# A decode step with attention and a gated MLP on one core: the MLP as one chain, w_out on 128 and 32 lanes, and output halves as alternate rows of one sum

## The chip, the cores and the metric

The kernel runs on one core of a Trainium2 chip. The metric is the device time of one execution in microseconds (us). Three runs of the kernel before gave 662.22, 662.27 and 662.43 us; the median is 662.27 us. About 0.2% of that, 1.3 us, is what a measurement of this kernel can tell from no change.

## What is computed

Four sequences (B = 4) decode one token each. The input `x` (4 x 640) is normalised; the result goes into an attention over a cache and, beside it, into a gated MLP; both are added to `x`:

```python
xn = layernorm(x)
q  = (xn @ wq) as 4 x 32 heads x 128
p  = softmax(q . k_cache / sqrt(128))        # k_cache, v_cache: 4 x 32 x 4096 x 128, bf16
A  = (p @ v_cache) as 4 x 4096 @ wo          # wo: 4096 x 640
z  = gelu(xn @ w_in)                         # w_in: 640 x 1728, so z is 4 x 2 x 864
B  = (z1 * (w_sp * layernorm(z2) + b_sp)) @ w_out   # w_out: 864 x 640
out = x + A + B                              # 4 x 640
```

The two caches (134 MB each) are nearly all of the bytes that have to be read.

## The kernel before, in words

**Work units.** The attention is cut into 16 units (`NU`): one sequence times eight heads (`hg` is the group of heads, `b` the sequence). The keys of a unit (8192 KB) and its values (8192 KB) are loaded so that each of the 128 partitions holds 64 KB in one run. A unit's keys come in four pieces (`NK`); a step `n` of the main loop handles one piece: VectorE multiplies it by the query in place (`product`, L514) and adds the upper half of the head dimension to the lower (`fold_half`, L520); TensorE adds the rest up with the identity as weights (`sums`, L529, eight matmuls); VectorE finishes the row sums (`row_sums`, L542). After four pieces come the maximum (`head_max`), the exponentials on ScalarE (`exps`, L564), and their spreading by head (`by_head`, L575). The weighted sum of the values is 64 matmuls a unit (`weighted`, L599).

**Places.** The keys live in a ring of seven slots of 2048 KB (`k_ring`), the values in one buffer of 8192 KB (`v_all`). Before the first values come, `v_all` holds the weights `wq`, `w_in` and the first five rows per lane of `w_out`; the other rows of `w_out` stand in `p_m`, which later holds the spread exponentials. `wo` goes into ring slot 4, a quarter of it per group of heads.

**Order.** PE, DVE, Activation and SP run in the written order (`manual_schedule`). All large loads are issued on SP from the list `loads`; `pump()` after each step issues the next ones whose places are free, and SP then waits at each for the readers of that place and for a free completion counter (there are eight, given out in turn). At the start ScalarE issues the load of `x` and five small loads with the last 96 rows of `w_out` (`w_end_sb`, 24 lanes, L115).

**The MLP.** `gmlp()` is a generator that the main loop advances with `next(mlp)`. The 864 features stand as six terms on 128 lanes and four on 24. Its 100 matmuls (L380) run in step 0; its VectorE and ScalarE pieces are dealt out over steps 1 and 2; its last part multiplies with `w_out` (L480: ten terms times two output halves, 20 matmuls).

**The output sum.** The 640 output columns are two halves of 320. Both are summed in one PSUM bank, `out_ps`: half 0 on partitions 0 to 3, half 1 on partitions 32 to 35 (`OG = 32`). Into it go `x` (L355), the MLP (L480), and four times a group of heads (`group_proj`, L668, 8 heads times 2 halves = 16 matmuls):

```python
def out_sum(half):
    return out_ps[OG * half : OG * half + Bsz, :]
...
nc.tensor.matmul(out=out_sum(half), lhsT=o, rhs=wo_sb[:, n, half * NOH : (half + 1) * NOH], ...)
```

**The end.** The last group's `wo` is loaded in six pieces (heads 0-1, 2-3, 4-5, 6, and head 7 in two halves), behind the last values, which come in five (the last four, L167, in falling sizes). After the last value piece: 16 matmuls into `o_last` (L778), their division on VectorE (L786), the 16 matmuls of `group_proj`, one copy of 36 partitions to SBUF on ScalarE (L792), and two stores of 4 x 320, one issued on ScalarE (L793) and one on SP (L794).

Of the kernel before, what the change touches and what calls it, by code (L numbers as in the profile page):

```python
# [9 lines left out]
FP32 = mybir.dt.float32  # L10
BF16 = mybir.dt.bfloat16
# [6 lines left out]
def kernel(  # L18
# [62 lines left out]
    once = ctx.enter_context(tc.tile_pool(name="once", bufs=1))  # L81
# [6 lines left out]

    pad.tile([P, 96], FP32, name="pad")

    p_m = const.tile([P, 2, NG, CB, HT], BF16, name="p_m")
    x_bf = const.tile([Bsz, D], BF16)
    nc.scalar.dma_start(out=x_bf[:], in_=A_x.flatten_outer_dims())

# [6 lines left out]
    w_in_sb = v_all[:, DC * HD : DC * (HD + F)].rearrange("p (c n) -> p c n", c=DC)  # L101


    NV = NFF - 1
    at_v = -(-DC * (HD + F) // 256) * 256
    w_out_sb = v_all[:, at_v : at_v + NV * D].rearrange("p (k n) -> p k n", k=NV)
    p_w = p_m[:].rearrange("p n g c h -> p (n g c h)")
    at_p = -(-D // 256) * 256
    w_row_sb = p_w[:, 0:D]
    w_end_sb = p_w[:, at_p : at_p + FR * D].rearrange("p (r n) -> p r n", r=FR)  # L110
    nc.sync.dma_start(out=wq_sb, in_=A_wq.rearrange("(p c) n -> p c n", c=DC))

    w_end_rows = B_w_out[NFF * P : Fh].rearrange("(p r) n -> p r n", r=FR)
    for l in range(LS):
        nc.scalar.dma_start(out=w_end_sb[l:FT:LS], in_=w_end_rows[l:FT:LS])  # L115

    def load_w():
        nc.sync.dma_start(out=w_in_sb, in_=B_w_in.rearrange("(p c) n -> p c n", c=DC))
        w_rows = B_w_out[0 : NFF * P].rearrange("(p k) n -> p k n", k=NFF)
# [54 lines left out]
    def wo_load(hg):  # L174
        return (lambda: load_wo(hg)), [WO_AT]

    loads = [k_load(0, 0, 2), (load_w, []), k_load(0, 2, 4), k_load(1)]
    for u in range(NU - 4):
        loads += [v_load(u), k_load(u + 2)]
        if u % Bsz == Bsz - 1:  # L180
# [164 lines left out]
        op1=ALU.add,  # L345
    )

    out_ps = ps_out.tile([P, NOH], FP32)
    OG = 32

    def out_sum(half):
        return out_ps[OG * half : OG * half + Bsz, :]

    for half in range(2):
        nc.tensor.matmul(  # L355
            out=out_ps[OG * half : OG * half + OG, :],
            lhsT=ident[:Bsz, :OG],
            rhs=x_bf[:, half * NOH : (half + 1) * NOH],
            start=True,
            stop=False,  # L360
        )

# [7 lines left out]
    gm["yT"] = work.tile([P, NFC, Bsz], BF16, name="yT")  # L370

    def gmlp():
        zz, gw, gt, gz = (gm[n] for n in ("zz", "gw", "gt", "gz"))
        zT = ps_pv.tile([P, 2, NFC, Bsz], FP32, tag="pv", name="zT")
        for t in range(2):
            f1 = t * Fh + NFF * P
            w_t = w_in_sb[:, :, t * Fh : f1].rearrange("p c (f k) -> p c k f", k=NFF)
            for k in range(NFC):
                for c in range(DC):
                    nc.tensor.matmul(  # L380
                        out=zT[: P if k < NFF else FT, t, k, :],
                        lhsT=w_t[:, c, k, :]
                        if k < NFF
                        else w_in_sb[:, c, f1 + k - NFF : f1 + FT * FR : FR],
                        rhs=xnT[:, c, 0:Bsz],
                        start=(c == 0),
                        stop=(c == DC - 1),
                    )
        yield
        nc.vector.tensor_copy(out=zz[:, :, 0:NFF, :], in_=zT[:, :, 0:NFF, :])  # L390
        nc.vector.tensor_copy(out=zz[:FT, :, NFF:], in_=zT[:FT, :, NFF:])
        nc.vector.tensor_tensor(out=gw[:], in0=zz[:], in1=zz[:], op=ALU.mult)
        nc.vector.tensor_scalar(
            out=gw[:], in0=gw[:], scalar1=0.044715, scalar2=1.0, op0=ALU.mult, op1=ALU.add
# [76 lines left out]
            in1=ac_sb[:, None, Bsz : 2 * Bsz].to_broadcast([P, NFC, Bsz]),  # L471
            op=ALU.add,
        )
        nc.vector.tensor_tensor(out=gm["yT"][:], in0=gz[:, 0, :, :], in1=sq, op=ALU.mult)
        w_terms = [w_out_sb[:, k] for k in range(NV)] + [w_row_sb]
        w_terms += [w_end_sb[:FT, r] for r in range(FR)]
        for k in range(NFC):
            w = P if k < NFF else FT
            for half in range(2):
                nc.tensor.matmul(  # L480
                    out=out_sum(half),
                    lhsT=gm["yT"][:w, k, :],
                    rhs=w_terms[k][:, half * NOH : (half + 1) * NOH],
                    start=False,
                    stop=False,
                )
# [151 lines left out]
    def group_turn(hg):  # L638
        rden = small.tile([P, 1], FP32, name="rden")
        nc.vector.reciprocal(out=rden[:], in_=rdens.pop(hg)[:])  # L640


        o_q = gr.pop(hg)[:].rearrange("p (q j) -> p q j", j=JR)
        o_n = once.tile([P, JR, PAR, QH], BF16, name="o_n")
# [9 lines left out]
        o_t = once.tile([P, JR, QD], BF16, name="o_t")  # L654
        nc.vector.transpose(
            out=o_t[:].rearrange("p j q -> p (j q)"),
            in_=o_n[:].rearrange("p j e q -> p (j e q)"),
        )
        o_s = once.tile([P, JR, Bsz], BF16, name="o_s")
        nc.vector.tensor_tensor(  # L660
            out=o_s[:], in0=o_t[:, :, 0:Bsz], in1=o_t[:, :, Bsz : 2 * Bsz], op=ALU.add
        )
        gr[hg] = [o_s[:, j, :] for j in range(JR)]

    def group_proj(hg):
        for n, o in enumerate(gr.pop(hg)):
            for half in range(2):
                nc.tensor.matmul(  # L668
                    out=out_sum(half),
                    lhsT=o,  # L670
                    rhs=wo_sb[:, n, half * NOH : (half + 1) * NOH],
                    start=False,
                    stop=(hg == HG - 1 and n == HT - 1),
                )
        busy.remove(WO_AT)

# [25 lines left out]
    with tc.manual_schedule(engines={E.PE, E.DVE, E.Activation, E.SP}):  # L702
# [74 lines left out]
        for c in range(NC):  # L777
# [4 lines left out]
                start=False,  # L782
                stop=(c == NC - 1),
            )
        o_n = small.tile([P, NQ, PAR, Bsz], BF16, name="o_n_last")
        nc.vector.tensor_tensor(out=o_n[:], in0=o_last[0][:], in1=rden[:], op=ALU.mult)  # L786
        gr[HG - 1] = [o_n[:, h // PAR, h % PAR, :] for h in range(HT)]
        group_proj(HG - 1)

        res = work.tile([P, NOH], BF16, name="res")  # L790
        out_v = out.flatten_outer_dims()
        nc.scalar.copy(out=res[0 : OG + Bsz], in_=out_ps[0 : OG + Bsz])  # L792
# [32 lines left out]
```

## Time and profile before

| what | value |
|---|---|
| device time, median of three runs | 662.27 us |
| span of the profiled execution | 660.5 us |
| median less span | 1.8 us |
| bytes read from HBM | 282.24 MB |
| DVE busy | 524.9 us (79%) |
| PE busy | 310.9 us (47%) |
| ACT busy | 29.8 us (5%) |
| chain that ended last | DMA 60%, DVE 30%, PE 9% |
| the last 16 matmuls of L668 | from 654.73 to 657.64 us |
| copy L792, then stores issued | 657.67 us, 658.12 us |

The page gives no time of its own for the profiled execution beside its span; the three timed runs are about 1.8 us longer than that span, which begins with the first instruction and ends with the last. "Busy" counts an engine's own work, not its waiting. The chain of waits goes back from the last instruction to whatever released each step. The granted clock is the share of full speed that TensorE got: 0.50 is half speed. The view by stretches of time prints, for each stretch, every engine's busy time, the granted clock, the mean busy share of the 16 DMA engines (a packet is booked where it starts, so short stretches can exceed 1.00) and the rate.

### The profile page before, as it was taken

The page shows a single profiled execution, that of the slowest core. Times are in us where ns is not written, and L with a number is a line of the kernel's source. Part 1 is how long each engine was busy: PE and PEld are TensorE (multiplying, and loading weights), DVE is VectorE, ACT ScalarE, POOL GpSimd, SP SyncE. Part 2 cuts the span into 40 slices and gives each one's busy share as a digit, 9 for nine tenths or more (in the row PEclk, how much of TensorE's full clock was granted, in tenths as well). Part 3 has the DMA queues.
Part 4 walks back from the last instruction along what each step waited for, and adds up shares of the span by engine and source line. Part 5 has one row for each costly group of instructions (what it writes and reads, how often), then busy time and mean ns, then how long its engine had stood idle before and what let it go on. Part 6 is the DMA issues. An engine that isn't in the chain of part 4 may idle for free.

```text
span 660.5 us, 4704 instructions
## 1 busy us (share of the span) xinstructions
PE 310.9 (47%) x2035; PEld 135.7 (21%) x2035; DVE 524.9 (79%) x332; ACT 29.8 (5%) x73; POOL 2.7 (0%) x12
## 2 busy tenths in 40 slices
PE   0274363526527362472536336362462633736366
PEld 0131122212203121130212112121130221212124
DVE  2578988959598795969959598695969969999950
ACT  0020000000000000000000000000000000000000
POOL 1000000000000000000000000000000000000000
PEclk9756686766768677576767768677576767678765
DMA  9999999999999999999999999999999999999997
GB/s 372 435 448 429 430 441 437 438 425 437 430 433 438 433 433 438 433 434 425 437 437 438 421 433 438 441 438 433 429 426 441 430 433 445 411 428 437 457 400 281
DMA packets 8113, 282.56 MB, mean 428 GB/s; under 512 B 888, under 2 KB 2180, under 8 KB 2588
## 3 DMA queue, kind: packets, MB, share of 16 engines
q1 hardware_dynamic: 8024, 282.12, 99.0%
q8 instruction: 16, 0.26, 0.1%
q10 hardware_dynamic: 68, 0.13, 0.1%
q14 instruction: 5, 0.04, 0.0%
HBM read 282.24 MB, written 0.01 MB: 427 GB/s over the span
## 4 chain that ended last, share of the span: by engine, by line
DMA 60%; DVE 30%; PE 9%; issue 1%; ACT 0%; DVEq 0%; SPq 0%
DMA k_ring<-in_A_k_cache_dram 52%; DVE k_ring L514 15%; DVE k_ring L520 8%; PE s_ps L529 7%; DMA v_all<-in_A_v_cache_dram 4%; DMA k_ring<-in_A_wo_dram 3%; DVE s_sb L542 2%; DVE p_m L575 1%; DVE m L551 1%; PE out_ps L668 1%; DVE o_n L646 1%; PE zT L380 1%; PE pv L599 1%; DVE mt L553 0%; PE out_ps L480 0%
## 5 line engine op out<-in xcount | busy, mean ns | idle before, releaser
L514 DVE TENSOR_TENSOR k_ring<-k_ring,qbc 128x8192 bf16<-128x8192 bf16 x64 | 282.7, 4418 | 86.3 <-DMA k_ring<-in_A_k_cache_dram 86.3
L529 PE MATMUL s_ps<-k_ring,ident 128*128 128x512 bf16 x512 | 201.1, 564 | 313.7 <-DVE k_ring L520 313.5
L529 PEld LDWEIGHTS <-ident 128*128 128x128 bf16 x512 | 65.4, 129 | 427.7 <-issue 383.7
L520 DVE TENSOR_TENSOR k_ring<-k_ring 128x4096 bf16<-128x4096 bf16 x64 | 145.9, 2279 | 0.0
L599 PE MATMUL pv<-v_all,p_m 128*32 128x512 bf16 x960 | 60.2, 407 | 0.0
L542 DVE TENSOR_REDUCE s_sb<-s_ps 128x64 f32<-128x512 f32 x64 | 43.6, 682 | 5.7 <-PE s_ps L529 5.7
L575 DVE TENSOR_TENSOR p_m<-p_c,own 128x2048 bf16<-128x2048 bf16 x16 | 36.5, 2284 | 0.7 <-ACT p_c L564 0.7
L599 PEld LDWEIGHTS <-p_m 128*32 128x32 bf16 x992 | 25.8, 103 | 39.4 <-issue 17.1
L564 ACT ACTIVATE p_c<-s_sb,nm 128x256 bf16<-128x256 f32 x16 | 8.1, 508 | 331.2 <-DVE nm L558 331.2
L630 PEld LDWEIGHTS o_ps<-o_rows,pick 128*128 128x128 f32 x96 | 19.5, 280 | 4.1 <-issue 3.0
L630 PE MATMUL o_ps<-o_rows,pick 128*128 128x128 f32 x96 | 18.6, 357 | 0.0
L611 ACT COPY o_rows<-pv 128x512 f32<-128x512 f32 x16 | 9.4, 586 | 167.4 <-PE pv L599 167.4
L293 DVE TENSOR_SCALAR q_rows<-q_ps 128x512 bf16<-128x512 f32 x2 | 1.4, 692 | 12.3 <-PE q_ps L285 12.3
L786 DVE TENSOR_TENSOR o_n_last<-o_last,rden_all 128x32 bf16<-128x32 f32 x1 | 0.2, 192 | 12.3 <-PE o_last L778 12.3
L504 ACT CAST qbc<-qbc_ps 128x128 bf16<-128x128 f32 x16 | 4.3, 266 | 101.7 <-PE qbc_ps L496 101.7
L285 PE MATMUL q_ps<-v_all,xnT 128*32 128x512 bf16 x40 | 4.3, 618 | 8.9 <-DMA v_all<-in_A_wq_dram 8.9
L551 DVE TENSOR_REDUCE m<-s_sb 128x1 f32<-128x256 f32 x16 | 6.7, 420 | 0.6
L496 PE MATMUL qbc_ps<-q_rows,of_row 128*128 128x128 bf16 x32 | 6.0, 277 | 0.6 <-DVE q_rows L293 0.6
L496 PEld LDWEIGHTS <-of_row 128*128 128x128 bf16 x32 | 4.2, 134 | 8.3 <-issue 7.8
L668 PE MATMUL out_ps<-k_ring,o_s 128*4 128x320 bf16 x48 | 4.4, 331 | 2.2 <-DVE o_s L660 2.2
L685 PE MATMUL o_last<-hot,o_rows 128*128 128x8 f32 x32 | 4.9, 280 | 0.7 <-ACT o_rows L611 0.7
L685 PEld LDWEIGHTS o_last<-hot,o_rows 128*128 128x128 f32 x32 | 4.8, 225 | 1.8 <-ACT o_rows L611 1.6
(89 smaller groups left out, 74.6 us busy)
## 6 DMA issues: line engine op xcount, KB each, us to landing
k_ring<-in_A_k_cache_dram SPq DMA_DIRECT2D x6, 4096.0 KB, 24.8
v_all<-in_A_v_cache_dram SPq DMA_DIRECT2D x2, 4096.0 KB, 28.8
v_all<-in_A_wq_dram SPq DMA_DIRECT2D x1, 5120.0 KB
k_ring<-in_A_v_cache_dram SPq DMA_DIRECT2D x1, 4096.0 KB
k_ring<-in_A_wo_dram SPq DMA_DIRECT2D x3, 1280.0 KB, 20.1
v_all<-in_B_w_in_dram SPq DMA_DIRECT2D x1, 2160.0 KB
k_ring<-in_A_v_cache_dram SPq DMA_DIRECT2D x1, 2048.0 KB
k_ring<-in_A_v_cache_dram SPq DMA_DIRECT2D x1, 1024.0 KB
```

The lines of the kernel that those rows point to most:

```text
L496: nc.tensor.matmul(out=qb_ps[:], lhsT=of_row[:, e, b].rearrange("p k f l -> p (k f l)"), rhs=q_rows[e][:, hg, :], start=(e == 0), stop=(e ...
L514: nc.vector.tensor_tensor(out=t, in0=t, in1=qbcs[u][:, None, :].to_broadcast([P, HC, Dh]), op=ALU.mult)
L520: nc.vector.tensor_tensor(out=t[:, :, 0:HD2], in0=t[:, :, 0:HD2], in1=t[:, :, HD2:Dh], op=ALU.add)
L529: nc.tensor.matmul(out=s[:], lhsT=ident[:], rhs=t[:, :, g * RW : (g + 1) * RW], start=(g == 0), stop=(g == m - 1),)
L542: nc.vector.tensor_reduce(out=scores[u][:, r * HC : (r + 1) * HC], in_=sums_ps.pop(n)[:], axis=AX.X, op=ALU.add,)
L551: nc.vector.tensor_reduce(out=m1[:], in_=scores[u][:], axis=AX.X, op=ALU.max)
L575: nc.vector.tensor_tensor(out=p_m[:, u % 2], in0=p_c.pop(u)[:].rearrange("p (g c) -> p g c", c=CB)[:, :, :, None].to_broadcast([P, NG, CB, HT]
L599: nc.tensor.matmul(out=pvs[u][cg * QD : (cg + 1) * QD, :], lhsT=p_m[:, u % 2, g0 + n].rearrange("p c h -> p (c h)"), rhs=v_at[:, n * CB : ...
L611: nc.scalar.copy(out=o[:].rearrange("p c d -> p (c d)"), in_=pvs.pop(u)[:])
L630: nc.tensor.matmul(out=gr[hg][:], lhsT=pick[:, c, Bsz - 1 - b : P + Bsz - 1 - b], rhs=o[:, c, :], start=(b == 0 and c == 0), stop=(b == Bs ...
L668: nc.tensor.matmul(out=out_sum(half), lhsT=o, rhs=wo_sb[:, n, half * NOH : (half + 1) * NOH], start=False, stop=(hg == HG - 1 and n == HT ...
L685: nc.tensor.matmul(out=o_last[0][:, :, :, u % Bsz], lhsT=o[:, c, :], rhs=hot[:, c, :].rearrange("p (k e) -> p k e", e=PAR), start=(c == 0) ...
```

## The change

Four things change together.

1. **Terms of the MLP.** The 864 features are now five terms on 128 lanes (`FA`) and seven on 32 (`FB`, `FL`): 12 terms in place of 10, so 120 matmuls with `w_in` and 24 with `w_out`. The 640 first rows of `w_out` are one load into `v_all`; the 224 others are four loads of 8 rows into `p_m` (`load_w_b`, on SP), behind the second half of the first keys. ScalarE's five small loads and SP's load of one row per lane are gone.
2. **First keys.** The first load of keys (two pieces, 4096 KB) is split in two of 2048 KB.
3. **One chain.** All of the MLP behind its first matmuls is done in step 1, after the second fold; `row_sums` of steps 0 and 1 stand between its parts. `v_all` is free for the first values after step 1 in place of step 2.
4. **Output sum.** `out_ps` has eight rows, row 2b + half. Each matmul has eight weight columns: a sequence's column stands at every second place of a tile with zeros between (`x_at`, `yT`, `o_s`, cleared by GpSimd at the start), and the two halves use the same tile shifted by one. All matmuls write partitions 0 to 7. One copy of eight partitions and one store of 8 x 320, issued on ScalarE, end the kernel.

Two small tiles of `group_turn` move into the end of `p_m`'s buffer. The diff, cut to what matters (`...` marks what is left out):

```diff
-    NFF = Fh // P
-    FR = 4
-    FT = (Fh - NFF * P) // FR
-    NFC = NFF + FR
-    LS = 5
+    FA, FL, LS = 5, 32, 4
+    FB = (Fh - FA * P) // FL
+    NFC = FA + FB
...
-    for l in range(LS):
-        nc.scalar.dma_start(out=w_end_sb[l:FT:LS], in_=w_end_rows[l:FT:LS])
+    def load_w_b():
+        for l in range(LS):
+            nc.sync.dma_start(out=w_b_sb[l:FL:LS], in_=w_b_rows[l:FL:LS])
...
-        nc.sync.dma_start(out=w_out_sb, in_=w_rows[:, 0:NV])
-        nc.sync.dma_start(out=w_row_sb, in_=w_rows[:, NV])
+        nc.sync.dma_start(
+            out=w_a_sb, in_=B_w_out[0 : FA * P].rearrange("(p k) n -> p k n", k=FA)
+        )
...
-    loads = [k_load(0, 0, 2), (load_w, []), k_load(0, 2, 4), k_load(1)]
+    loads = [k_load(0, 0, 1), k_load(0, 1, 2), (load_w, []), k_load(0, 2, 4), (load_w_b, []), k_load(1)]
...
-    out_ps = ps_out.tile([P, NOH], FP32)
-    OG = 32
-    def out_sum(half):
-        return out_ps[OG * half : OG * half + Bsz, :]
+    OR = 2 * Bsz
+    out_ps = ps_out.tile([OR, NOH], FP32)
+    def at_half(w, half):
+        return w[:, 1 - half : 1 - half + OR]
...
-                    out=out_sum(half),
-                    lhsT=o,
+                    out=out_ps[:],
+                    lhsT=at_half(o, half),
                     rhs=wo_sb[:, n, half * NOH : (half + 1) * NOH],
                     start=False,
-                    stop=(hg == HG - 1 and n == HT - 1),
+                    stop=(hg == HG - 1 and n == HT - 1 and half == 1),
...
-            if n in (1, 2):
-                next(mlp)
-            if n:
+            if n > 2:
                 row_sums(n - 1)
...
             if n == 1:
                 next(mlp)
-            if n in (1, 2):
+                row_sums(0)
                 next(mlp)
...
-            if n == 2:
+            if n == 1:
+                next(mlp)
+                row_sums(1)
+                next(mlp)
+                next(mlp)
                 busy.remove(V)
...
-        nc.scalar.copy(out=res[0 : OG + Bsz], in_=out_ps[0 : OG + Bsz])
-        nc.scalar.dma_start(out=out_v[:, 0:NOH], in_=res[0:Bsz])
-        nc.sync.dma_start(out=out_v[:, NOH:D], in_=res[OG : OG + Bsz])
+        nc.scalar.copy(out=res[:], in_=out_ps[:])
+        nc.scalar.dma_start(
+            out=out.flatten_outer_dims().rearrange("b (h n) -> (b h) n", h=2), in_=res[:]
+        )
```

More of the change, by code (lines that the diff above doesn't have):

```diff
@@ L346 @@
     )
-    out_ps = ps_out.tile([P, NOH], FP32)
-    OG = 32
-    def out_sum(half):
-        return out_ps[OG * half : OG * half + Bsz, :]
+    OR = 2 * Bsz
+    out_ps = ps_out.tile([OR, NOH], FP32)
+    def at_half(w, half):
+        return w[:, 1 - half : 1 - half + OR]
+    x_at = const.tile([Bsz, OR + 1], BF16, name="x_at")
+    nc.gpsimd.memset(x_at[:], 0.0)
+    nc.gpsimd.tensor_copy(out=x_at[:, 1::2], in_=ident[:Bsz, :Bsz])
+    yT = const.tile([P, NFC, OR + 1], BF16, name="yT")
+    nc.gpsimd.memset(yT[:], 0.0)
+    o_s = const.tile([P, JR, OR + 1], BF16, name="o_s")
+    nc.gpsimd.memset(o_s[:], 0.0)
     for half in range(2):
         nc.tensor.matmul(
-            out=out_ps[OG * half : OG * half + OG, :],
-            lhsT=ident[:Bsz, :OG],
+            out=out_ps[:],
+            lhsT=at_half(x_at, half),
             rhs=x_bf[:, half * NOH : (half + 1) * NOH],
-            start=True,
+            start=(half == 0),
             stop=False,
@@ L369, with lanes @@
     gm["ac"] = work.tile([1, 2 * Bsz], FP32, name="ac")
-    gm["yT"] = work.tile([P, NFC, Bsz], BF16, name="yT")
+    def lanes(k):
+        return P if k < FA else FL
     def gmlp():
@@ L375, in gmlp @@
         for t in range(2):
[L376 to L377 removed]
+            w_t = w_in_sb[:, :, t * Fh : (t + 1) * Fh]
             for k in range(NFC):
+                w_k = (
+                    w_t[:, :, k : FA * P : FA]
+                    if k < FA
+                    else w_t[:, :, FA * P + k - FA : Fh : FB]
+                )
                 for c in range(DC):
                     nc.tensor.matmul(
[L381 to L384, printed above, removed]
+                        out=zT[0 : lanes(k), t, k, :],
+                        lhsT=w_k[:, c],
                         rhs=xnT[:, c, 0:Bsz],
@@ L389, in gmlp @@
         yield
-        nc.vector.tensor_copy(out=zz[:, :, 0:NFF, :], in_=zT[:, :, 0:NFF, :])
-        nc.vector.tensor_copy(out=zz[:FT, :, NFF:], in_=zT[:FT, :, NFF:])
+        nc.vector.tensor_copy(out=zz[:, :, 0:FA, :], in_=zT[:, :, 0:FA, :])
+        nc.vector.tensor_copy(out=zz[:FL, :, FA:], in_=zT[:FL, :, FA:])
         nc.vector.tensor_tensor(out=gw[:], in0=zz[:], in1=zz[:], op=ALU.mult)
@@ L473, in gmlp @@
         )
-        nc.vector.tensor_tensor(out=gm["yT"][:], in0=gz[:, 0, :, :], in1=sq, op=ALU.mult)
-        w_terms = [w_out_sb[:, k] for k in range(NV)] + [w_row_sb]
-        w_terms += [w_end_sb[:FT, r] for r in range(FR)]
+        nc.vector.tensor_tensor(out=yT[:, :, 1::2], in0=gz[:, 0, :, :], in1=sq, op=ALU.mult)
+        w_terms = [w_a_sb[:, k] for k in range(FA)] + [w_b_sb[:, r] for r in range(FB)]
         for k in range(NFC):
-            w = P if k < NFF else FT
             for half in range(2):
                 nc.tensor.matmul(
-                    out=out_sum(half),
-                    lhsT=gm["yT"][:w, k, :],
+                    out=out_ps[:],
+                    lhsT=at_half(yT[0 : lanes(k), k], half),
                     rhs=w_terms[k][:, half * NOH : (half + 1) * NOH],
@@ L653, in group_turn @@
             )
-        o_t = once.tile([P, JR, QD], BF16, name="o_t")
+        o_t = p_end[:, JR * QD : 2 * JR * QD].rearrange("p (j q) -> p j q", j=JR)
         nc.vector.transpose(
-            out=o_t[:].rearrange("p j q -> p (j q)"),
-            in_=o_n[:].rearrange("p j e q -> p (j e q)"),
+            out=p_end[:, JR * QD : 2 * JR * QD], in_=p_end[:, 0 : JR * QD]
         )
-        o_s = once.tile([P, JR, Bsz], BF16, name="o_s")
         nc.vector.tensor_tensor(
-            out=o_s[:], in0=o_t[:, :, 0:Bsz], in1=o_t[:, :, Bsz : 2 * Bsz], op=ALU.add
+            out=o_s[:, :, 1::2], in0=o_t[:, :, 0:Bsz], in1=o_t[:, :, Bsz : 2 * Bsz], op=ALU.add
         )
-        gr[hg] = [o_s[:, j, :] for j in range(JR)]
+        gr[hg] = [o_s[:, j] for j in range(JR)]
     def group_proj(hg):
@@ L668, in group_proj @@
                 nc.tensor.matmul(
-                    out=out_sum(half),
-                    lhsT=o,
+                    out=out_ps[:],
+                    lhsT=at_half(o, half),
                     rhs=wo_sb[:, n, half * NOH : (half + 1) * NOH],
                     start=False,
-                    stop=(hg == HG - 1 and n == HT - 1),
+                    stop=(hg == HG - 1 and n == HT - 1 and half == 1),
                 )
@@ L784 @@
             )
-        o_n = small.tile([P, NQ, PAR, Bsz], BF16, name="o_n_last")
-        nc.vector.tensor_tensor(out=o_n[:], in0=o_last[0][:], in1=rden[:], op=ALU.mult)
-        gr[HG - 1] = [o_n[:, h // PAR, h % PAR, :] for h in range(HT)]
-        group_proj(HG - 1)
-        res = work.tile([P, NOH], BF16, name="res")
-        out_v = out.flatten_outer_dims()
-        nc.scalar.copy(out=res[0 : OG + Bsz], in_=out_ps[0 : OG + Bsz])
-        nc.scalar.dma_start(out=out_v[:, 0:NOH], in_=res[0:Bsz])
-        nc.sync.dma_start(out=out_v[:, NOH:D], in_=res[OG : OG + Bsz])
+        nc.vector.tensor_tensor(
+            out=o_s[:, :, 1::2],
+            in0=o_last[0][:].rearrange("p k e b -> p (k e) b"),
+            in1=rden[:].rearrange("p k e b -> p (k e) b"),
+            op=ALU.mult,
+        )
+        gr[HG - 1] = [o_s[:, h] for h in range(HT)]
+        group_proj(HG - 1)
+        res = work.tile([OR, NOH], BF16, name="res")
+        nc.scalar.copy(out=res[:], in_=out_ps[:])
+        nc.scalar.dma_start(
+            out=out.flatten_outer_dims().rearrange("b (h n) -> (b h) n", h=2), in_=res[:]
+        )
 _INS = ['A_x', 'A_k_cache', 'A_v_cache', 'A_wq', 'A_wo', 'B_x', 'B_w_in', 'B_w_sp', 'B_b_sp', 'B_w_out']
```

20 lines of the change are left out of this document (9 added, 11 removed).

## The prediction, made before the changed kernel ran

> **What bounds the kernel now.** I read the stretches of time first, because the chain of waits gives DMA 60% but DVE 30%, and a chain can run through an engine that holds nothing up.
>
> ```profile
> 1.00:41.00 40.00, 13.30 (x159) 7.81 (x159) 15.87 (x22) 3.39 (x5) 2.20 (x7) 0.79 1.00 419
> 41.00:81.00 40.00, 18.05 (x58) 6.34 (x59) 36.72 (x40) 4.17 (x8) 0.00 (x0) 0.59 1.02 439
> 81.00:121.00 40.00, 19.22 (x110) 8.42 (x110) 34.47 (x19) 1.45 (x4) 0.00 (x0) 0.67 1.00 433
> 121.00:621.00 500.00, 235.50 (x1435) 100.50 (x1434) 421.33 (x240) 18.63 (x51) 0.00 (x0) 0.70 1.00 433
> 621.00:655.00 34.00, 22.39 (x265) 11.79 (x264) 16.32 (x15) 1.77 (x4) 0.00 (x0) 0.65 0.98 413
> ```
>
> The second number from the right is the busy share of the DMA engines: 1.00 from 1 us on, to within a few us of the end. Packet by packet the trace says the same: a 64 KB packet takes 2.418 us on its engine, in any stage, and the next starts at once; I found no pause of 0.2 us on any of the 16 engines between the first packet (1.7 us) and their last loads. So work on DVE and PE costs nothing as long as the queues never run dry. What can move the time is the bytes of the slowest DMA engine, a queue that runs dry, and what follows the last landings. That end I read next, in the chain of waits from 600 us on (start, length, what):
>
> ```profile
> 607.98 26.36 DMA v_all<-in_A_v_cache_dram
> ...
> 634.36 21.95 DMA k_ring<-in_A_wo_dram
> ...
> 656.35 1.30 PE out_ps L668 x8
> ...
> 657.67 0.42 ACT res L792
> ```
>
> Then the last matmuls one by one in the timeline of PE:
>
> ```profile
> 654.73 0.43 PE L668 MATMUL out_ps<-k_ring,o_n_last 128*4 128x320 bf16 x2 [0.28 <-DVE o_n_last L786]
> 656.35 0.43 PE L668 MATMUL out_ps<-k_ring,o_n_last 128*4 128x320 bf16 x2 [0.17 <-DMA k_ring<-in_A_wo_dram]
> 656.57 0.48 PE L668 MATMUL out_ps<-k_ring,o_n_last 128*4 128x320 bf16 x2
> ```
>
> "x2" is the point. The two halves of a head start 3 to 7 ns apart and run side by side; the next pairs start at 656.57, 656.84 and 657.11. A pair costs 0.267 us, not each matmul. PE keeps step with the landings of `wo`: the pairs at 655.49 and 656.35 waited for theirs, and so did the very last half (657.21). The last packet of `wo` lies at 656.8 us.
>
> **The change part by part.**
>
> *Output rows (the part that costs).* Both halves now write partitions 0 to 7, with eight weight columns each. Within one half, before, successive heads write the same partitions and start 0.267 us apart (0.22 only for the first behind a pause; 0.136 in the group at 389.11, at full clock). I take that as the step between any two matmuls to the same rows: 0.267 us at the clock of 0.50 which the end gets. Bounds: the halves still overlap (0.133 each) or not at all (0.267); the row for two matmuls on the same partitions is the nearer one, so 0.267. Their weight loads (80 to 129 ns) lie under the product before, as they do now. The tail then is 16 x 0.267:
> - it starts where it starts now, 654.73, behind the division L786 (0.19 us; its output has a stride now, I add nothing);
> - the last of 16 starts 15 x 0.267 = 4.01 us later, at 658.73. The pieces of `wo` all land before their turn (the last at 657.2), so PE bounds the tail, not the landings;
> - before, the last one started at 657.21. Both ends add the same 0.43 us. Cost: 658.73 - 657.21 = **+1.52 us**.
>
> The other places are covered. `group_proj` of the first three groups grows from 1.25 us (16 at full clock) or 1.85 us (230.87) to 2.2 to 4.3 us. Behind it on SP stands a load of keys that needs slot 4 (issued 232.76 and 390.40), which comes up to 2.4 us later. Those loads land 26.9 and 28.0 us after their issue, and 8192 KB at 433 GB/s take 19.4, so more than 7 us of other bytes are queued ahead: hidden. On PE, the next `sums` wait for a product and a fold anyway (4.42 + 2.28 us).
>
> *One copy, one store.* The copy reads 320 numbers on eight partitions in place of 36: 0.42 us as now, since the free size is the same. Two stores become one of eight rows. ScalarE's store is seen done at 659.43, SP's at 659.61, so at most 0.18 us goes; a store of eight rows may take as much longer as the issue of 5-row loads (0.62 to 0.79 us) does over that of this 4-row store (0.28), but a 128-row issue takes 0.33. Bounds -0.2 and +0.3; I take **-0.1**, nearest to the two stores themselves.
>
> *w_out and first keys on the DMA engines.* By the packet records: before, 24 rows of 5120 B came five at a time, on at most five engines (up to 5 x 0.196 us each), and 128 rows of 1280 B on all (8 x 0.055). That is 1.42 us on the loaded engines and 0.44 on the others. Now 32 rows of 8960 B come eight at a time: four on each of eight engines, each between 0.309 (8192 B) and 0.385 (10240 B), say 0.338, so 1.35 us, and nothing on the other eight. The split keys replace 8 x 1.213 by 16 x 0.611 us, +0.07 everywhere. The loaded engines stay at 1.42. Others gain 0.37 or lose 0.98, and which of them ends last I can't tell. Bounds -0.4 and +1.0; I take **0.0**, the value for the engines loaded in both.
> [...]
>
> *One chain, earlier start.* The first piece of keys now lands about 4.8 us earlier (2048 KB at 433 GB/s), so the first product starts when the query is ready (22.1) in place of 26.11. The fold and `sums` follow (2.28 + 3.57): SP issues the second keys near 32.5, not 36.52. Then 120 matmuls of 0.042 us (L380) to about 38, the MLP's vector pieces, `sums` of step 1 in between, and 24 products of `w_out` at 0.267 (6.4 us, not 2.92), from about 47.5 to 54. The ten that read `v_all` are done near 50.4, where SP may issue the first values: 56.92 before. Step 2 starts near 47.5 in place of 55.25. Every load is issued earlier than now, at queues that didn't run dry before. The four small loads stand ahead of the second keys on SP; each waits for a completion counter of a load that has landed by about 27 us, before 32.5. **0.0**: nothing waits for the gain. Without that cover (queues dry at 56 us) it would be worth up to the 6 us by which the values come earlier.
>
> Sum against the profiled execution: 660.5 + 1.52 - 0.1 + 0.0 = 661.9. Times stand 1.8 us above that span: 662.27 + 1.42 = **663.7 us**, 0.21% slower.
>
> [...]
>
> **Rivals.**
>
> *The clock is released in the tail* (not slower). Rows: in the group at 389.11, 16 matmuls as eight pairs took 1.25 us at full clock. Sixteen single ones at 0.136 would start within 15 x 0.136 = 2.0 us, by 656.8, before the last landing at 657.2; then the landings bound the tail again and only the -0.1 stays: 662.2. For it: after `sums` began at 568.95, 586.57 and 600.84 the granted clock rose to 1.00 within 3.3 to 4.5 us, and the tail is now dense. Against: the products of L778 kept PE 90% busy from 648 to 652 us and the clock stayed at 0.50. It decides by when the release comes: at 658.0, the earliest by those delays, about 0.4 us is saved (663.3); from 0.1 us saved on the result is within 0.2%; for 662.2 it must come by about 656.
> [...]
>
> *A newly loaded DMA engine ends last*: +0.98 before the tail, so 664.7; the opposite, 663.3. Against the extreme: the ends differ by 3 us between engines, so one has to be near the last already.
>
> *A queue that runs dry early*, if the single-file products or small loads hold up the first values beyond 60 us: some us slower. Nothing in the order says so.
>
> *The start matters after all* (a hidden gap): up to 6 us faster. The packet records speak against it.
>
> **How the numbers follow.** Forecast (serial tail at half clock, 663.2 to 664.2): 0.58. Clock released in the tail or halves partly together (662.2 to 663.2): 0.20. DMA engine or small fetches later (664.2 to 664.9): 0.14. Dry queue 0.04, faster start 0.04. The range from 662.4 to 664.8 leaves out the last two and the ends of the others, about 0.15. The bound of 0.2% (1.32 us, about what a measurement can tell from no change) is at 663.6, inside the forecast: about 0.4 of its 0.58 lies above it. Slower 0.40 + 0.14 + 0.04 = 0.58; faster 0.04; within 0.38.
>
> **What would show it.** Right: 16 matmuls of the last `group_proj` start 0.267 us apart and end near 659.2, without waiting for `wo`; the first values are issued about 6 us earlier and the DMA share still reads 1.00 throughout. Wrong: starts in pairs; a clock of 1.00 after 658; a last landing of the values' pieces that differs from 653.8 by more than 0.5 us; a DMA share under 0.95 in the first 80 us.

## The result, and the profile after

The changed kernel takes **664.10 us** (median of nine runs, 663.52 to 664.55); the kernel before took 662.27 us beside it (nine runs, 662.19 to 662.55). The ratio is 1.0024, with an interval of 1.0016 to 1.0033: slower by 1.8 us. The forecast was 663.7 us. The profiled execution has a span of 661.7 us (660.5 before) and a device time of 663.52 us, so it is the shortest of the nine; this matters below.

The stretches of time of the changed kernel, with the columns that the prediction showed (busy time and count of PE, PEld, DVE, ACT and POOL, granted clock, DMA share, GB/s):

```profile
1.00:41.00 40.00, 15.54 (x181) 9.75 (x181) 20.35 (x30) 4.95 (x7) 2.59 (x11) 0.78 0.99 416
41.00:81.00 40.00, 20.12 (x64) 7.54 (x63) 34.88 (x31) 2.62 (x7) 0.00 (x0) 0.71 1.01 438
81.00:121.00 40.00, 18.32 (x109) 7.77 (x108) 32.53 (x18) 1.45 (x4) 0.00 (x0) 0.67 1.02 440
121.00:621.00 500.00, 238.94 (x1433) 103.45 (x1431) 420.77 (x240) 18.63 (x51) 0.00 (x0) 0.70 1.00 433
621.00:655.00 34.00, 22.44 (x262) 11.07 (x260) 16.70 (x15) 1.77 (x4) 0.00 (x0) 0.65 0.98 412
```

The DMA share is what it was, 0.98 to 1.02 in every stretch, although DVE's work has moved forward (20.35 us of it by 41 us, 15.87 before). The queues of large loads were full before the change and they still are. The early start shows in the timeline of SP, which issues the second keys (L146) and the first values (L157). First the changed kernel, then the first values in the kernel before:

```profile
31.98 0.34 SPq L146 DMA_DIRECT2D k_ring<-in_A_k_cache_dram  x1
50.20 0.33 SPq L157 DMA_DIRECT2D v_all<-in_A_v_cache_dram  x1
```

```profile
56.92 0.33 SPq L157 DMA_DIRECT2D v_all<-in_A_v_cache_dram  x1
```

The values are issued 6.7 us earlier, and nothing of it reaches the end. The end itself, in the chain of waits (start, length, what):

```profile
612.48 41.82 DMA k_ring<-in_A_v_cache_dram
...
654.34 0.61 PE o_last L787 x16
...
654.98 0.21 DVE o_s L794
...
655.23 3.77 PE out_ps L675 x16
...
659.02 0.42 ACT res L804
```

Before, the chain ran through `wo` up to 656.31 and then through eight products. Now `wo` is no longer in it: it goes from the last values through the division and then through all 16 products in one unbroken run. The first and the last of these in the timeline of PE:

```profile
655.23 0.69 PE L675 MATMUL out_ps<-k_ring,o_s 128*8 128x320 bf16 x2 [0.29 <-DVE o_s L794]
```

```profile
657.86 1.13 PE L675 MATMUL out_ps<-k_ring,o_s 128*8 128x320 bf16 x6
```

Behind the first step of 0.22 us the starts are 0.267 us apart (one by one in the trace: 655.46, 655.72, 655.99 and so on to 658.12); then come 658.28, 658.41, 658.55 and 658.69, 0.136 apart. Six products begin within 0.83 us in the second fence, which single file at 0.267 would not allow. The stretches of PE alone (PE busy, granted clock, DMA share, GB/s) say why:

```profile
656.00:657.00 1.00, 1.00 (x5) 0.50 0.19 63
657.00:658.00 1.00, 1.00 (x5) 0.50 0.02 7
658.00:659.00 1.00, 0.98 (x7) 0.92 0.00 0
```

The clock came back at 658.16 (0.92 is the mean of 0.16 us at 0.50 and 0.84 us at 1.00). Term by term, in us:

| in the profiled runs | before | changed |
|---|---|---|
| start of the last group of `o_last` | 653.85 | 654.34 |
| first of the 16 products | 654.73 | 655.23 |
| start of the last one | 657.21 | 658.69 |
| its end | 657.64 | 658.99 |
| end of the copy to end of the span | 2.39 | 2.30 |
| span | 660.49 | 661.74 |

From first to last start it is 2.485 us before and 3.455 now: +0.97. In the profile of e6, below, where the clock stayed at 0.50, it is 3.96 us; so the clock saved 0.50 us here. The tail starts 0.50 us later, which the prediction had at zero, so that in this profile the two cancel.

### The profile page after: what moved, and what is told of

It reads as the page before. It is cut to its first block, busy times and chain, and to the rows that moved or that the text cites. A ratio compares the mean times of both kernels' runs of the same rounds, so it can differ in the third digit from the quotient of the medians.

```text
span 661.7 us, 4753 instructions
## 1 busy us (share of the span) xinstructions
PE 319.1 (48%) x2059; PEld 141.3 (21%) x2059; DVE 525.6 (79%) x332; ACT 29.8 (5%) x73; POOL 3.1 (0%) x16
## 4 chain that ended last, share of the span: by engine, by line
DMA 62%; DVE 29%; PE 8%; issue 1%; SPq 0%; ACT 0%; DVEq 0%
DMA k_ring<-in_A_k_cache_dram 53%; DVE k_ring L523 15%; DVE k_ring L529 7%; DMA k_ring<-in_A_v_cache_dram 6%; PE s_ps L538 6%; DMA v_all<-in_A_wq_dram 2%; DVE s_sb L551 2%; DVE p_m L584 1%; PE out_ps L675 1%; DVE m L560 1%; PE q_ps L285 1%; DVE p_m L655 1%; DVE mt L562 1%; DVE mt L565 0%; DVE nm L567 0%
## 5 line engine op out<-in xcount | busy, mean ns | idle before, releaser
L675 PE MATMUL out_ps<-k_ring,o_s 128*8 128x320 bf16 x64 | 11.2, 336 | 2.2 <-DVE o_s L667 1.9
L675 PEld LDWEIGHTS <-o_s 128*8 128x8 bf16 x64 | 5.8, 96 | 7.1 <-DVE o_s L667 2.7
L393 PE MATMUL zT<-xnT,v_all 128*32 128x4 bf16 (+1 forms) x120 | 6.2, 188 | 0.0
L393 PEld LDWEIGHTS <-v_all 128*32 128x32 bf16 (+1 forms) x120 | 6.2, 141 | 0.0
```

What stands on the lines that cost most here:

```text
L393: nc.tensor.matmul(out=zT[0 : lanes(k), t, k, :], lhsT=w_k[:, c], rhs=xnT[:, c, 0:Bsz], start=(c == 0), stop=(c == DC - 1),)
L675: nc.tensor.matmul(out=out_ps[:], lhsT=at_half(o, half), rhs=wo_sb[:, n, half * NOH : (half + 1) * NOH], start=False, stop=(hg == HG - 1 a ...
```

## The experiments

All were run in three groups, each beside the kernel before on the same chip, whose medians were 662.33 (18 runs), 662.31 (22) and 662.27 us (19). Times are medians with their extremes. "Lost DMA time" below is the time that packets of SP's queue took beyond what a packet of that size usually takes, as a mean over the 16 engines. It is added up from the packet records of the traces and stands in no view.

**e1, the changed kernel without the output rows.** Halves on partitions 0 and 32 again, two stores; all else is as changed.

```diff
+    def out_sum(half):
+        return out_ps[OG * half : OG * half + Bsz, :]
+    def cols(w):
+        return w[:, 1:OR:2]
...
-                    out=out_ps[:],
-                    lhsT=at_half(o, half),
+                    out=out_sum(half),
+                    lhsT=cols(o),
```

> The changed kernel with its output halves put back on partitions 0 and 32 (four weight columns each, two copies' rows, two stores); first keys, w_out split and MLP chain stay as changed. Theory (single-file products in the tail cost the time): the last pairs wait for wo again, starts in pairs 0.27 us apart, and the time falls from 664.1 by 1.2 to 1.8 us, to between 662.3 and 662.9; the upper end if the last landings stay about 0.5 us later than before, as in the profile of the changed kernel, the lower end if that was chance. Rival (the MLP chain, the split keys or the new w_out loads cost it): stays near 664.

Measured: 662.70 us (662.46 to 662.91), ratio 1.0003 (0.9994 to 1.0011). The 16 products in the timeline of PE are pairs again (two of them begin 2 to 7 ns apart, all but the last two); first the first pair, then all 16:

```profile
655.08 0.43 PE L679 MATMUL out_ps<-k_ring,o_s 128*4 128x320 bf16 x2 [0.29 <-DVE o_s L798]
```

```profile
655.08 2.92 PE L679 MATMUL out_ps<-k_ring,o_s 128*4 128x320 bf16 x16 [0.29 <-DVE o_s L798]
```

They take 2.92 us in all, first start to last end, with pauses for `wo`; single file they took 3.77 with the clock's help. With the rows away no slowdown above the interval is left: of the 1.83 us between the medians 1.40 went with the rows, and 0.37 that the interval does not tell from nothing stayed.

**e2, the kernel before with the output rows alone** (rows 2b + half, shifted tiles, one copy, one store; loads and MLP as before).

```diff
...
-                    out=out_sum(half),
-                    lhsT=o,
+                    out=out_ps[:],
+                    lhsT=at_half(o, half),
...
```

> The kernel before with only the output rows and the one store of the change (loads, MLP terms and chain as before). Theory: the 16 last products start singly 0.267 us apart from 654.7 on, +1.52 us, less up to 0.55 us where the clock of TensorE is released on the way, less 0.2 us for the store: 663.0 to 663.6. Rival (the loads and the chain cost the time, the rows nothing): 662.0 to 662.3.

Measured: 664.09 us (663.64 to 665.53), ratio 1.0029 (1.0019 to 1.0039). That is 0.5 us above the range that was expected, and as much as the whole change. Its chain of waits ends with

```profile
654.27 0.61 PE o_last L783 x16
...
655.16 4.45 PE out_ps L673 x16
```

Here the clock returned only at 659.85, and the 16 products took 4.45 us, 0.68 more than in the profile of the changed kernel. From first to last start it is 3.96 us, +1.47 over the kernel before. The other 0.4 us is a later tail: its last group of `o_last` starts at 654.27 in place of 653.85. The rows have a second place in this kernel, the products with `w_out` in the old order of the MLP. First the ten that read `v_all` in e2 and the issue of the first values behind them, then the same ten in the kernel before:

```profile
55.24 2.83 PE L486 MATMUL out_ps<-v_all,yT 128*8 128x320 bf16 x10 [2.94 <-DVE yT L480]
...
58.10 0.33 SPq L157 DMA_DIRECT2D v_all<-in_A_v_cache_dram  x1
```

```profile
55.39 1.50 PE L480 MATMUL out_ps<-v_all,yT 128*4 128x320 bf16 x10 [2.72 <-DVE yT L474]
```

In single file they free `v_all` later, and the first values are issued 1.2 us later than before. In the packet records the DMA engines are then idle for 0.13 us on average between 60.5 and 62 us, where the kernel before has no gap, and 17 packets of 64 KB that start between 59.1 and 63.4 take 2.51 to 3.38 us in place of 2.418. Of the lost DMA time of e2 between 50 and 150 us (0.54 us, 0.11 in the kernel before) 0.43 us lies there. Idle and lost time together, 0.56 us, agree with the later tail in size; this is read from one profile and was not tested by a run.

**e6, the changed kernel once more, and e8, the kernel before once more** (no edit; second profiles of both).

> The changed kernel once more, for a second profile of its tail and its time on the chip of these runs. If its spread (663.5 to 664.6) comes from where the clock of TensorE is released among the 16 products: the step between products is 0.267 us up to the release and 0.136 us behind it, and the profiled run's time moves with it, by up to 0.55 us. Rival (the spread comes from the landings): products alike in both profiles and the last landing of values moves.

> The kernel before once more, for a second profile. If the last values land up to 0.5 us apart from run to run by chance: the last group of L778 starts between 653.8 and 654.4. If the later landings of the changed kernel come from its loads: again 653.8 to 653.9.

Measured: e6 664.04 us (663.33 to 664.11), ratio 1.0022 (1.0012 to 1.0032); e8 662.16 us in one run, span 660.37. The last group of `o_last` starts at 654.27 in e6 and at 653.73 in e8, which is what e8 was expected to show if the loads of the change delay the landings. The profiled run of e6 took 664.11 us, and its stretches of PE read

```profile
657.00:658.00 1.00, 1.00 (x5) 0.50 0.01 3
658.00:659.00 1.00, 1.00 (x5) 0.50 0.00 0
659.00:660.00 1.00, 0.59 (x3) 0.50 0.00 0
660.00:661.00 1.00, 0.00 (x0) 0.98 0.02 5
```

```profile
655.16 4.43 PE L675 MATMUL out_ps<-k_ring,o_s 128*8 128x320 bf16 x16 [0.29 <-DVE o_s L794]
```

The clock stayed at 0.50 to 660.03, behind the last product. So the two profiles of one kernel show the two cases that the prediction had set apart. Without the clock's help the serial term can be read whole: first to last start is 3.96 us in e6 and 2.49 in e8, **+1.47** (forecast +1.52). The spans differ by 1.95 us: +0.55 from the later start of the tail (655.16 against 654.61), +1.47, +0.04 in the last product and -0.11 behind the copy.

**e7, two stores of four rows** in place of one of eight, on ScalarE and SP.

```diff
-        nc.scalar.dma_start(
-            out=out.flatten_outer_dims().rearrange("b (h n) -> (b h) n", h=2), in_=res[:]
-        )
+        out_v = out.flatten_outer_dims().rearrange("b (h n) -> (b h) n", h=2)
+        nc.scalar.dma_start(out=out_v[0:Bsz], in_=res[0:Bsz])
+        nc.sync.dma_start(out=out_v[Bsz:OR], in_=res[Bsz:OR])
```

> The changed kernel with two stores of four rows, on ScalarE and SP, in place of one of eight rows; all else as changed. Theory (one store saves the later end of two): 0.1 to 0.25 us slower than the changed kernel, 664.2 to 664.4, seen as the time from the end of the copy to the end of the span. Rival (eight rows take as long as two stores): no difference.

Measured: 664.03 us (663.65 to 664.09), ratio 1.0024 (1.0014 to 1.0034). It was expected to be slower, at 664.2 to 664.4; in the device time the store cannot be told from no change. In the profiles, end of copy to end of span is 2.37 to 2.57 us in the seven runs with two stores (before, e1, e5, e7, e8, e9, e11) and 2.21 to 2.34 in the seven with one (changed, e2, e3, e4, e6, e10, e12). The medians are 0.15 us apart, about as forecast; e7, whose stores alone differ from those of the changed kernel, has 2.37 against 2.30 and 2.29, so 0.07 to 0.08. The profile of e7 is also a third one of the single-file tail: 3.96 us from first to last start, and the clock stays at 0.50 to the end of the span at 662.29.

**e10, twice the products, single file.** In the last group each product has one with zero weights (`o_z`) ahead of it, which adds nothing to the sum.

```diff
...
+            for half in range(2 if hg == HG - 1 else 0):
+                nc.tensor.matmul(
+                    out=out_ps[:],
+                    lhsT=at_half(o_z, half),
+                    rhs=wo_sb[:, n, half * NOH : (half + 1) * NOH],
+                    start=False,
+                    stop=False,
+                )
```

> The changed kernel, and in the last group each of the 16 output products has one more ahead of it with zero weights, which adds nothing to the sum: 32 products in single file. Theory (products to the same eight rows follow each other, 0.267 us apart at the clock of 0.50 and 0.136 at full clock, and PE alone bounds the tail): in the two profiles of the changed kernel the clock came back 2.9 and 4.9 us after the first product of the tail. 4 us at 0.267 are 15 products, the other 17 at 0.136 take 2.3 us, so the last one starts about 6.3 us behind the first in place of 3.0 to 4.0: 2.0 to 2.8 us over the changed kernel, about 666.4; 4.3 us, 668.3, if the clock does not come back. Rival (the tail is bound by the landings of wo or by what each product waits for, not by the products): less than 0.5 us more, 664.1 to 664.6.

**e11, the same in pairs**: e1 with a zero pair ahead of each pair.

> The changed kernel with the halves on partitions 0 and 32 and two stores (as in e1), and in the last group each pair of products has a pair with zero weights ahead of it: again 32 products, but as 16 pairs. Theory (a pair takes the time of one product): 16 pairs are as long as the 16 single products of the changed kernel, so 662.7 + 1.5 = 664.2 us (663.6 if the clock comes back early), and 2 to 2.8 us below the same 32 products in single file. Rival (it is the number of products or the bytes they read that counts, and the pairs of before were only waiting for wo): the time of the 32 in single file, about 666.4.

Measured: e10 665.45 us (665.26 to 666.00), ratio 1.0048 (1.0034 to 1.0062); e11 664.10 us (663.57 to 664.38), ratio 1.0025 (1.0015 to 1.0034). From the timeline of PE, first e10, then e11 (here the zero products are L677 and L681):

```profile
656.49 0.74 PE L685 MATMUL out_ps<-k_ring,o_s 128*8 128x320 bf16 x2
657.03 0.74 PE L677 MATMUL out_ps<-k_ring,o_z 128*8 128x320 bf16 x2
...
660.07 0.43 PE L677 MATMUL out_ps<-k_ring,o_z 128*8 128x320 bf16 x2
660.34 0.43 PE L685 MATMUL out_ps<-k_ring,o_s 128*8 128x320 bf16 x2
```

```profile
656.46 0.48 PE L689 MATMUL out_ps<-k_ring,o_s 128*4 128x320 bf16 x2
656.72 0.48 PE L681 MATMUL out_ps<-k_ring,o_z 128*4 128x320 bf16 x2
...
658.86 0.48 PE L681 MATMUL out_ps<-k_ring,o_z 128*4 128x320 bf16 x2
659.12 0.48 PE L689 MATMUL out_ps<-k_ring,o_s 128*4 128x320 bf16 x2
```

Two products to the same rows take 0.53 to 0.54 us at the clock of 0.50 (656.49 to 657.03) and 0.27 at full clock; two products to rows on partitions 0 and 32 (e11) take 0.26 to 0.27 at 0.50, from end to end of the run. The same number of products, reading the same bytes of `wo`, is 1.35 us shorter in pairs, and 16 pairs (664.10) are as long as the 16 single products of the changed kernel (664.10 and 664.04); from first to last start 16 pairs take 3.96 us in e11 and 16 single products 3.96 in e6. So the cost follows the place of the output, not the count of the products or their reads. The two also differ in weight columns, eight in single file and four in pairs. No run has eight columns with the halves on partitions 0 and 32; but with four columns successive pairs, which go to the same rows again, start 0.267 us apart in e11 (655.390, 655.657, 655.924), the step that eight columns have, so the number of columns does not set it. The size for e10 was missed: +1.4 us over the changed kernel and not 2.0 to 2.8, since the clock came back earlier than in either profile I had reckoned from, at 657.67, 2.7 us behind the first product, and 20 of the 31 steps were at 0.136. For the same reason e11 is 1.35 us below e10 and not 2 to 2.8; its own time, 664.2, was met.

**e5, the loads of the kernel before evened out**: the last 96 rows of `w_out` on 96 lanes as one load, in place of 24 lanes in five loads.

```diff
-    FR = 4
+    FR = 1
...
-    LS = 5
+    LS = 1
```

> The kernel before with the last 96 rows of w_out as one term on 96 lanes in place of four on 24: one load of 96 rows of 1280 B for five loads of 24 rows of 5120 B; 70 and 14 matmuls of the MLP, not 100 and 20. Every DMA engine then moves 6 rows (0.33 us), where up to five engines moved 5 rows of 5120 B (0.98 us) and the others none. If the loaded engines end last in the kernel before: up to 0.65 us faster, 661.7 to 662.1. Rival (others end last, or engines even out): from no change to 0.33 us slower, 662.2 to 662.6.

Measured: 662.36 us (662.11 to 663.59), ratio 1.0004 (0.9995 to 1.0013). The few engines reckoned to carry 1.42 us of small loads (5 x 0.196 + 8 x 0.055) were not the ones that the end waited for, or evening them is worth less than 0.1%.

**e9, e1 with even loads** (six terms on 128 lanes, one on 96; one load of 96 rows).

```diff
-    FA, FL, LS = 5, 32, 4
+    FA, FL, LS = 6, 96, 1
...
-            out=w_a_sb, in_=B_w_out[0 : FA * P].rearrange("(p k) n -> p k n", k=FA)
+        nc.sync.dma_start(out=w_a_sb, in_=w_rows[:, 0 : FA - 1])
+        nc.sync.dma_start(out=w_row_sb, in_=w_rows[:, FA - 1])
```

> As e1 (changed kernel with pairs and two stores), but with w_out on 128 and 96 lanes: six terms and one, one load of 96 rows in place of four of eight, and one row per lane by its own load, as before. Theory A (the 0.4 us that e1 has over the kernel before come from the DMA engines that the small loads load more): 662.3. Theory B (they come from the split of the first keys or from the order of the loads): 662.7. Theory C (they are chance): anything between.

Measured: 662.55 us (662.33 to 662.73), ratio 1.0003 (0.9994 to 1.0012). It falls between theories A and B, as C (chance) allowed, and with this noise it rules none of them out. The last wait for `wo` ends at 656.35 before, 656.18 in e5, 656.69 in e1 and here at

```profile
634.46 21.98 DMA k_ring<-in_A_wo_dram
...
656.48 1.28 PE out_ps L681 x8
```

The last values differ with them, by up to 0.5 us; no experiment ties this to one part of the change.

**e3, the changed kernel with two loads of 16 rows, and e12, with one of 32**, in place of four of eight.

```diff
-    FA, FL, LS = 5, 32, 4
+    FA, FL, LS = 5, 32, 2
```

> The changed kernel with the 32 rows of w_out loaded as two loads of 16 rows in place of four of 8, so that each row goes to another DMA engine: 2 rows on each of 16 engines, 0.68 us, not 4 rows on 8, 1.35 us. If the load of those engines delays the last landings: landings and time earlier by 0.3 to 0.7 us, 663.4 to 663.8. Rival (the 0.5 us in the landings is chance, or the loaded engines don't end last): 664.1, within 0.2.

> The changed kernel with one load of 32 rows of w_out in place of four of eight: 16 engines, two rows each, all at once. Theory A (16 engines that write into the same 32 partitions slow each other, which made e3 with its two loads slower): packets of 8960 bytes of 0.37 us and more, slow packets behind them, 664.7 us or more. Theory B (it was the order of the two loads, one behind the other, or chance): packets of 0.34 us, no lost engine time, 663.6 to 664.2.

Measured: e3 664.91 us (664.17 to 665.04), ratio 1.0035 (1.0022 to 1.0047); e12 664.75 us (663.93 to 665.03), ratio 1.0033 (1.0020 to 1.0046). These loads were meant to lie evenly on sixteen engines, and the time goes up, against both expectations of e3. The stretch around these loads, first in the changed kernel, then in e3, then in e12:

```profile
41.00:46.00 5.00, 3.36 (x11) 1.04 (x9) 2.18 (x11) 0.31 (x2) 0.00 (x0) 0.72 1.21 523
```

```profile
41.00:46.00 5.00, 3.89 (x10) 1.15 (x10) 1.79 (x9) 0.59 (x2) 0.00 (x0) 0.63 1.27 455
```

```profile
41.00:46.00 5.00, 3.49 (x10) 1.04 (x8) 2.18 (x11) 0.40 (x2) 0.00 (x0) 0.70 1.25 452
```

The DMA engines are busier (1.27 and 1.25 against 1.21) and move less (455 and 452 GB/s against 523). The packets of 8960 bytes all take 0.338 us with four loads; with two they have a median of 0.373 and reach 0.644, with one 0.443 and 0.664, and 16 or 17 of the 64 KB packets near them take up to 3.6 and 3.7 us in place of 2.418. The lost DMA time between 30 and 50 us is 1.12 and 1.09 us, against 0.03 in the changed kernel. The last group of `o_last` starts 0.68 us later in e12 (655.02 against 654.34) and 0.26 later in e3. So the loss repeats, and two loads in a row are not its cause, since one load has it too; the medians alone (0.65 and 0.8 us over the changed kernel, with ranges that overlap) would not show it. That the short rows are what slows the 64 KB packets is not shown: most of the loss is in these, and in e4, below, 16 such packets are slowed about as much with no more than four short rows at a time. What slows the short rows themselves, to 0.644 and 0.664 us, no run shows either.

**e4, eight loads of four rows.**

```diff
-    FA, FL, LS = 5, 32, 4
+    FA, FL, LS = 5, 32, 8
```

> The changed kernel with the same rows as eight loads of 4 rows: 8 rows on each of four engines, 2.7 us in place of 1.35. If the load of an engine goes straight into the end of the stream: up to 1.35 us later, 664.8 to 665.5. Rival (engines even out, or other engines end last): 664.1 to 664.4.

Measured: 667.12 us (666.27 to 667.28), ratio 1.0067 (1.0053 to 1.0081). It lies far above both expectations: it was meant as a dose of loaded engines and became something else. SP's timeline and the stretch behind it:

```profile
25.73 17.94 SPq L115 DMA_DIRECT2D p_m<-in_B_w_out_dram  x6
43.80 0.35 SPq L146 DMA_DIRECT2D k_ring<-in_A_k_cache_dram  x1
```

```profile
41.00:46.00 5.00, 3.67 (x10) 1.15 (x10) 1.96 (x10) 0.58 (x2) 0.00 (x0) 0.67 0.78 270
```

The last of the small loads is not issued before 43.09; the waits of SP name pieces of keys as what held this line up (18.0 us in three waits, the longest 9.7). A completion counter still in use would fit this, but was not shown. The second keys stand behind it on SP and are issued at 43.80 in place of 31.98. The queues then run dry (DMA share 0.78 against 1.21), and the whole kernel is 3 us later. The packet records have 2.9 us of idle per engine between 41 and 50 us (none in the changed kernel). Behind it the first 16 packets of 64 KB of the second keys begin within 0.41 us of each other, from 44.77 on, and take 2.85 to 3.46 us in place of 2.418; the lost DMA time between 30 and 50 us is 0.8 us. That prices the rival "a queue that runs dry early": 2.9 us of idle and 0.8 us of lost time per engine became 3.0 us.

## Why the prediction was right, and where it was off

- **Output rows, +1.52.** Right in kind and size: single file, 0.267 us apart at the clock of 0.50, no wait for `wo`; +1.47 where the clock stayed down, since the first step behind the pause is 0.22 us. Shown by e1 (away without them), e2 (there with them alone) and e10 with e11 (the place of the output, not the number of products).
- **Clock released in the tail** (a rival, 663.3 at 658.0). The prediction had a clock of 1.00 after 658 as a sign of being wrong, and it did come in one of three profiles of this tail: at 658.16 in the profile of 663.52 us, not before the last product in those of 664.11 (e6) and 664.07 (e7). In the trace of the changed kernel the changes of the clock lie 3.41 us apart or a multiple of it (647.92, 651.33, 658.16, 661.57), and its place against the tail differed from run to run: 2.9 us behind the first product in this profile, 4.9 in e6. That the spread of the changed kernel (663.33 to 664.55) comes from this was only argued; these three profiles agree with it. The 0.50 us saved in the one profile are a third of the term; for the whole of it the clock would have had to come by 656 by the prediction's estimate, which no run showed.
- **The tail starts where it did, 654.73.** This is the step that was off, by size. The tail started at 655.23 and 655.16 in the two profiles of the changed kernel, and at 654.73 and 654.61 in those of before: 0.5 us, about the amount by which 664.1 exceeds 663.7. The last packet of the values ends at 653.94 and 653.76, against 653.47 and 653.35. I had booked "newly loaded DMA engine" between -0.4 and +1.0 and taken 0.0, the value for engines loaded in both kernels. No run shows this term: the packet records name no engine, so which ones the two kernels load stays unknown, and the runs showed the later start in its place. The last group of `o_last` starts between 654.13 and 654.35 us in all six profiles with the changed loads (changed, e1, e6, e7, e10, e11) and between 653.73 and 653.85 in three of the four profiles with the old order of the loads (before, e5, e8); the fourth, e2 at 654.27, had its queues run dry. So chance alone is unlikely, and 0.3 to 0.6 us go with the changed loads and their order. Which of them it is stays open: e9, with the new order and even loads, starts at 653.97, between the two groups, and e1, which keeps the changed loads, is slower than before by 0.37 us in device time, inside the uncertainty.
- **One store, -0.1.** About right by the profiles (0.07 to 0.15 us), too small for the device times (e7).
- **Earlier chain, 0.0.** Right. The first product started at 21.58 (22.1 forecast), the second keys were issued at 31.98 (32.5) and the first values at 50.20 (50.4), and the DMA share is still full. e4 shows the other side: the cover is needed, and a chain on SP that was late by 12 us cost 3 us. And e2 shows that with the output rows the early start is needed as cover: in the old order the first values come 1.2 us later than before, at 58.10, and the queues run dry for a moment, the prediction's rival, which the changed kernel escapes.
- **Sum.** Forecast +1.42 us, measured +1.83 between the medians. The two parts tried alone (e1 +0.37, e2 +1.76) add up to 2.13; without the 0.4 us by which e2 starts its tail later they make 1.7, the same within their uncertainty. In the profiled run the forecast's sum came near for a wrong reason in part: the span is 661.7 us, close to the 661.9 that the forecast adds up to, but there the late start (+0.50) and the clock's help (-0.50) cancel.

## What to carry to other kernels

Before outputs are packed into fewer rows of an accumulator, look whether products to different rows start together in the timeline: here a pair on partitions 0 and 32 cost one product (0.267 us at the clock of 0.50), and packing both into rows 0 to 7 lengthened the stretch in which PE sets the end from 2.49 to 3.96 us, to save about 0.1 us at a store. Work that started earlier behind full DMA queues brought nothing by itself here (the first values were issued 6.7 us earlier and the tail began 0.5 us later), though it covered a delay elsewhere (in e2, without it, the first values came 1.2 us later than before), while small loads that waited ahead of a large one on SP cost far more than their bytes (e4: the same 0.29 MB in eight loads, 3.0 us over the changed kernel). Judge how small loads are spread by the times of the packets, not by the balance of the engines alone: two loads of 16 rows and one of 32, meant to lie evenly, took 0.8 and 0.65 us more than four of eight (e3, e12).

## What the runs showed of the hardware that was not expected

- Where the 32 short rows came in two loads of 16 or one of 32 (e3, e12), these rows were slower (up to 0.664 us in place of 0.338), and so were 64 KB packets near them (up to 3.7 us in place of 2.418): 1.1 us of lost time per engine for 0.29 MB, where four loads of eight lost 0.03. The 64 KB packets were slow in e4 as well, with no more than four short rows at a time: 16 that began within 0.41 us of each other behind a dry queue took 2.85 to 3.46 us. What the two cases share stays open.
- The granted clock came back between 2.5 us (e12) and 4.9 us (e6) behind the first product of a tail without pauses, and in e7, with the same tail, not before the end of the span, 7.2 us behind it. In e1, where the products wait for `wo`, it did not come back in the tail at all.
